# Top-k attention and a SwiGLU FFN in one kernel: units by query tile, FFN blocks of 256 tokens across batches, V stationary, mask and SwiGLU products on GpSimd, tanh for sigmoid

## The chip, the core and the metric

The kernel runs on one NeuronCore of a Trainium2 chip. Its engines are TensorE (PE, with its weight loads listed as PEld), VectorE (DVE), ScalarE (ACT), GpSimd (POOL) and SyncE (SP), which here only issues DMAs. The metric is the device time of one execution in microseconds (us). Before the change it is 2606.95 us, the median of 3 runs (2606.77 to 2609.73).

## What is computed

Everything is float32. Attention over 8 batches, 8 heads, 576 tokens and 64 dimensions per head keeps the 32 largest scores of each row; its output, with the heads side by side, is a matrix x of 4608 tokens by 512, which goes through a SwiGLU block with 1536 hidden columns. The three FFN weights arrive as float64.

```python
scores = scale * np.matmul(q, k.transpose(0, 1, 3, 2))          # scale = 1/8
kth = np.partition(scores, -32, axis=-1)[..., -32:-31]
scores = np.where(scores >= kth, scores, -1e9)
attn = np.exp(scores - np.max(scores, axis=-1, keepdims=True))
attn = attn / (np.sum(attn, axis=-1, keepdims=True) + 1e-09)
x = np.matmul(attn, v).transpose(0, 2, 1, 3).reshape(4608, 512)
g = x @ w_gate
out = (g * (1.0 / (1.0 + np.exp(-g))) * (x @ w_val)) @ w_out
```

## The kernel before

**Units.** Attention goes by unit. A unit is one batch, one pair of heads and one tile of queries: four tiles of 128 queries (two heads, so 256 rows of 576 scores), and a last one of 64 queries, in which both heads share one tile of 128 rows. I call the first kind a full unit and the last kind a half unit. There are 160 units, 128 full and 32 half. The order is batch, pair of heads, tile of queries: a pair's five units follow each other (L188).

**One unit.** `scores` (L195) multiplies Q by K for the 512 main keys and the last 64 of each head, and ACT copies the scores from PSUM (L211). `select` (L214) finds the 32nd largest of each row with four MAX8 (L227) and three MATCH_REPLACE8 (L237) on DVE; POOL makes -scale*max (L229), ACT the exponential of every score (L231), and DVE zeroes what lies below the threshold (L240, one scalar_tensor_tensor per head: compare, then multiply). `turn` (L250) transposes the result on PE (L260, L266) and ACT copies it out (L261, L267). `values` (L275) multiplies it with V: the transposed weights of 128 queries are the stationary operand and 65 columns of V (64 and a column of ones, which gives the row's sum) are streamed past it (L287). DVE adds epsilon to the sum and inverts it (L295, L296), ACT scales (L299), PE transposes once more (L303) and ACT copies into xT (L306).

**FFN.** `feed` (L316) is a generator for one batch in three blocks of 192 tokens (BLK). Each of the 12 slabs of hidden columns is one piece: four products with w_gate into PSUM and a copy by ACT (L336); after all 12 the sigmoid on ACT over 2304 columns (L338) and one product of that size on POOL (L339); then 12 pieces with w_val, multiplied on DVE straight from PSUM (L341). Last come the output products (L348), with 512 streamed columns each. A block of 192 tokens is cut at the 128-token tiles, so every block has one output tile of 128 tokens and one of 64.

**Order of the work.** The main loop (L368) emits for each unit n: scores of n+1, selection of n, transposes of n-1, four pieces of `feeds` (L381), and the values of n-2. A batch's FFN enters `feeds` when its last unit is done, so it runs beside the units of the next batch. At the start `feeds` holds `weights` (L127): 72 pieces which each load 128 by 256 float64 numbers by a DMA from POOL's queue (L91) and round them on POOL, ACT and DVE (L97 to L122), also four per unit. `load` (L145) issues 12 DMAs for a pair from SP's queue; `prep` (L158) transposes K and Q, and POOL copies V beside its ones (L184, L185).

The program order sets priorities and not the order on an engine: the tile framework lays the order of each engine out ahead of time by priority and expected readiness, and the order then stays fixed. In the trace PE runs two gate or value products between the transposes of L260 and L266, which the program has later.

```python
sc = work.tile([P, 2, S], ...)      # 2 buffers; PSUM: ps_s 2 x 2 banks, ps_t 2, ps_f 2
per_unit = 4                        # pieces of FFN, or of weights, behind each unit
```

Of the kernel before, what the change touches and what calls it, by code (L numbers as in the profile page):

```python
# [9 lines left out]
ALU = mybir.AluOpType  # L10
# [6 lines left out]
LOWEST = -3.4028234663852886e38  # L17
EPS = 1.0e-9
BLK = 192
WP = 256  # L20
HUGE = 122880.0  # 1151 << 20 as a float32's bits
LEAST = 3.4332275390625e-05  # 897 << 20 as a float32's bits
# [3 lines left out]
def kernel(  # L26
# [10 lines left out]
    """Top-k attention, then SwiGLU, in float32 throughout.  # L37

    Attention goes by unit (batch, pair of heads, tile of queries): the scores
    of both heads, the 32nd largest of each row by four rounds of max and three  # L40
    of match_replace, exp(s - max) zeroed below it, and the product with the
    values, whose last column of ones gives the sum of the row. A pair of heads
    is one 128-row slab of x transposed, which is what the first products of
    the FFN want. The FFN of a batch runs between the units of the next one.

    The tokens of a head are laid out as 4 tiles of the tokens 4 p + j, j < 4,
    and a last one of 64, so that each partition reads 1 KiB in one piece.

    The weights come in float64 and are rounded to float32 here, on their bits,
    while the first batch's attention runs.  # L50
    """
# [9 lines left out]
    DE = D + 1  # L61
    scale = 1.0 / float(D) ** 0.5
    assert D == 64 and R == 64 and H * D == DM and DM == 512 and S % BLK == 0

    consts = ctx.enter_context(tc.tile_pool(name="consts", bufs=1))
    ld = ctx.enter_context(tc.tile_pool(name="ld", bufs=2))
    work = ctx.enter_context(tc.tile_pool(name="work", bufs=2))
    small = ctx.enter_context(tc.tile_pool(name="small", bufs=4))
    conv = ctx.enter_context(tc.tile_pool(name="conv", bufs=2))
    ffn = ctx.enter_context(tc.tile_pool(name="ffn", bufs=2))  # L70
    ps_s = ctx.enter_context(tc.tile_pool(name="ps_s", bufs=2, space=PSUM))
    ps_t = ctx.enter_context(tc.tile_pool(name="ps_t", bufs=2, space=PSUM))
    ps_f = ctx.enter_context(tc.tile_pool(name="ps_f", bufs=2, space=PSUM))
# [3 lines left out]
    NV = 3  # L77
    vbufs = []
    for i in range(NV):
        vt = consts.tile([P, 2, J + 1, DE], FP32, name=f"v{i}")  # L80
        nc.gpsimd.memset(vt[:], 1.0)
        vbufs.append(vt)
# [4 lines left out]
    def rounded(src, dst):  # L87
        """Float64 bits, [low, high] word by word, to the nearest float32."""
        n = dst.shape[1]
        w = conv.tile([P, n, 2], I32, tag="w", name="w")  # L90
        nc.gpsimd.dma_start(w[:], src.bitcast(I32).rearrange("p (f t) -> p f t", t=2))  # L91
        yield
        low, high = w[:, :, 0], w[:, :, 1]
        # As float32 numbers the high words have the order of the float64 ones.
        # Held to float64 exponents up to 1151, float32's infinity.
# [4 lines left out]
        size = conv.tile([P, n], FP32, tag="size", name="size")  # L100
        nc.scalar.activation(size[:], hi[:], AF.Abs)
        # From 896 to 1151 the exponents' top bit and low seven are float32's exponent.
# [13 lines left out]
        half = conv.tile([P, n], I32, tag="half", name="half")  # L116
# [4 lines left out]
        # Zero below the exponent 897, that of float32's least normal number.  # L121
# [5 lines left out]
    def weights():  # L127
        pieces = []
        for src, dst in ((w_gate, wg), (w_val, wv), (w_out, wo)):
            for c in range(dst.shape[1]):  # L130
                for f in range(0, dst.shape[2], WP):
                    pieces.append(
                        rounded(src[c * P : (c + 1) * P, f : f + WP], dst[:, c, f : f + WP])
                    )
        for n in range(len(pieces) + 1):
            if n < len(pieces):
                next(pieces[n])
            if n > 0:
                next(pieces[n - 1], None)
                yield  # L140
# [4 lines left out]
    def load(i):  # L145
        b, hp = pairs[i]
        raw[i] = {}
        for name, src in (("k", k), ("q", q), ("v", v)):
            t = ld.tile([P, J + 1, 2, D], FP32, tag=name, name=f"{name}_in")
            for hh in range(2):  # L150
                head = src[b, 2 * hp + hh]
                nc.sync.dma_start(
                    t[:, 0:J, hh, :], head[0:JP].rearrange("(p j) d -> p j d", j=J)
                )
                nc.sync.dma_start(t[0:R, J, hh, :], head[JP:S])
            raw[i][name] = t

    def prep(i):  # L158
        """K and Q transposed, both heads in one slab; V beside its ones."""
        got = raw.pop(i)  # L160
        slabs = []
        for name in ("k", "q"):
            slab = work.tile([P, S], FP32, tag=name + "T", name=name + "T")
            main = ps_t.tile([P, 512], FP32, tag="t", name="main")
            for c in range(J):
                nc.tensor.transpose(
                    main[:, c * P : (c + 1) * P],
                    got[name][:, c].rearrange("p h d -> p (h d)"),
                    ident[:],
                )  # L170
            nc.scalar.copy(slab[:, 0:JP], main[:])
            slabs.append(slab)
        last = ps_t.tile([P, 512], FP32, tag="t", name="last")
        for n, name in enumerate(("k", "q")):
            nc.tensor.transpose(
                last[:, n * R : (n + 1) * R],
                got[name][0:R, J].rearrange("p h d -> p (h d)"),
                ident[0:R, 0:R],
            )
        for n, slab in enumerate(slabs):  # L180
            nc.scalar.copy(slab[:, JP:S], last[:, n * R : (n + 1) * R])
        vb = vbufs[i % NV]
        to = vb[:, :, :, 0:D].rearrange("p h j d -> p j h d")
        nc.gpsimd.tensor_copy(to[:, 0:J], got["v"][:, 0:J])  # L184
        nc.gpsimd.tensor_copy(to[0:R, J], got["v"][0:R, J])  # L185
        preps[i] = (*slabs, vb)

    units = [(i, qt) for i in range(len(pairs)) for qt in range(J + 1)]  # L188
    state = {}

    def n_tiles(qt):
        """The last 64 queries of both heads share one tile."""
        return 1 if qt == J else 2

    def scores(n):  # L195
        i, qt = units[n]
        kT, qT, _ = preps[i]
        sc = work.tile([P, 2, S], FP32, tag="sc", name="sc")
        ql = R if qt == J else P
        tiles = [(0, 1)] if qt == J else [(0,), (1,)]  # L200
        for t, heads in enumerate(tiles):
            ps = ps_s.tile([P, 1024], FP32, tag="s", name="s")
            for x, hh in enumerate(heads):
                d = slice(hh * D, (hh + 1) * D)
                for k0, k1 in ((0, 512), (512, S)):
                    nc.tensor.matmul(  # L206
                        ps[x * R : x * R + ql, k0:k1],
                        qT[d, qt * P : qt * P + ql],
                        kT[d, k0:k1],
                    )  # L210
            nc.scalar.copy(sc[:, t, :], ps[:, 0:S])  # L211
        state[n] = dict(sc=sc)
# [209 lines left out]
```

## Time and profile before

| | |
|---|---|
| time, median of 3 runs | 2606.95 us |
| span of the profiled execution, first to last instruction | 2599.7 us |
| median run less that span | 7.2 us |
| busy share of PE, DVE, ACT, POOL | 89%, 74%, 37%, 12% |
| mean granted clock of TensorE | 0.976 |
| first unit's first MAX8 | at 15.8 us |
| first MAX8 of each batch | 15.8, 365, 637, 927, 1217, 1508, 1798, 2088 us |
| last rounded weight written | at 356 us |
| HBM traffic over the span | 47.19 MB read, 9.44 MB written |

Of the profiled execution only the span is known; its own time from launch to end is not listed, so the 7.2 us between the span and the median run stand for what lies around it. In the profile a busy share counts the time in which an engine has an instruction in flight. Matmuls overlap in their pipeline, so the mean duration of one (349 ns at 192 columns) is not what one costs in a row of them; for that the start-to-start times are used. A float32 product shows as two MATMUL records. Batches 2 to 6 follow each other every 290.0 us.

### The profile page before, as it was taken

The page shows a single profiled execution, that of the slowest core. Times are in us where ns is not written, and L with a number is a line of the kernel's source. Part 1 is how long each engine was busy: PE and PEld are TensorE (multiplying, and loading weights), DVE is VectorE, ACT ScalarE, POOL GpSimd, SP SyncE. Part 2 cuts the span into 40 slices and gives each one's busy share as a digit, 9 for nine tenths or more (in the row PEclk, how much of TensorE's full clock was granted, in tenths as well). Part 3 has the DMA queues.
Part 4 walks back from the last instruction along what each step waited for, and adds up shares of the span by engine and source line. Part 5 has one row for each costly group of instructions (what it writes and reads, how often), then busy time and mean ns, then how long its engine had stood idle before and what let it go on. Part 6 is the DMA issues. An engine that isn't in the chain of part 4 may idle for free. (4 is left out here: it accounts for less than half of the span.)

```text
span 2599.7 us, 33003 instructions
## 1 busy us (share of the span) xinstructions
PE 2325.9 (89%) x12160; PEld 1733.6 (67%) x12160; DVE 1911.0 (74%) x4136; ACT 971.4 (37%) x2108; POOL 314.3 (12%) x473
## 2 busy tenths in 40 slices
PE   5656579999999999999999999999999999999898
PEld 3444456667767668668667668668668667677666
DVE  7889898778787788769777788769768788765000
ACT  3333234335334335334434434434425434423111
POOL 3434321011011011011001001001101101000000
PEclk9999998999999999999999999999999999999999
DMA  3222110000000000000000000000000000000000
GB/s 100 61 67 71 62 34 14 21 17 19 21 19 17 20 7 19 16 21 15 21 20 15 21 16 19 7 20 15 21 20 15 21 16 1 7 7 5 7 5 11
DMA packets 128032, 58.75 MB, mean 23 GB/s; under 512 B 118656, under 2 KB 118656, under 8 KB 127872
## 3 DMA queue, kind: packets, MB, share of 16 engines
q1 hardware_dynamic: 122112, 37.78, 6.0%
q0 software_dynamic: 5760, 18.88, 2.4%
q8 instruction: 96, 1.57, 0.3%
q14 instruction: 64, 0.52, 0.1%
HBM read 47.19 MB, written 9.44 MB: 22 GB/s over the span
## 5 line engine op out<-in xcount | busy, mean ns | idle before, releaser
L227 DVE MAX8 m<-rest 128x8 f32<-128x576 f32 x864 | 619.8, 748 | 1.7
L326 PE MATMUL f<-xT,wv 128*128 128x192 f32 x2304 | 459.3, 349 | 76.1 <-DVE h L341 75.9
L348 PE MATMUL f<-wo,h 128*128 128x512 f32 (+1 forms) x1152 | 506.6, 595 | 0.0
L326 PEld LDWEIGHTS f<-xT,wv 128*128 128x128 f32 x2304 | 400.0, 203 | 99.0 <-DVE h L341 85.0
L287 PE MATMUL av<-v,et 128*128 128x65 f32 (+3 forms) x3200 | 455.4, 287 | 3.2 <-ACT et L261 3.0
L287 PEld LDWEIGHTS av<-v,et 128*128 128x128 f32 (+3 forms) x3200 | 417.4, 195 | 58.1 <-issue 14.1
L326 PE MATMUL f<-xT,wg 128*128 128x192 f32 x2304 | 419.6, 331 | 6.5 <-ACT g L336 6.5
L237 DVE MATCH_REPLACE8 rest<-m,rest 128x576 f32<-128x576 f32 x576 | 424.5, 742 | 0.0
L326 PEld LDWEIGHTS f<-xT,wg 128*128 128x128 f32 x2304 | 370.8, 191 | 22.1 <-ACT g L336 10.7
L348 PEld LDWEIGHTS f<-wo,h 128*128 128x128 f32 (+1 forms) x1152 | 183.0, 163 | 291.2 <-issue 288.1
L206 PE MATMUL s<-kT,qT 64*128 64x64 f32 (+3 forms) x1280 | 297.9, 483 | 84.3 <-ACT sc L211 84.1
L211 ACT COPY sc<-s 128x576 f32<-128x576 f32 x288 | 182.1, 642 | 438.1 <-PE s L206 323.4
L295 DVE TENSOR_SCALAR rinv<-av 128x2 f32<-128x2 f32 (+1 forms) x160 | 25.0, 156 | 358.2 <-PE av L287 351.2
L206 PEld LDWEIGHTS s<-kT,qT 64*128 64x128 f32 (+1 forms) x1280 | 154.2, 193 | 184.3 <-ACT sc L211 88.8
L231 ACT ACTIVATE e<-sc,bias 128x576 f32<-128x576 f32 x288 | 213.3, 771 | 166.8 <-POOL bias L229 166.3
L240 DVE SCALAR_TENSOR_TENSOR e<-sc,m,e 128x576 f32<-128x576 f32 x288 | 273.2, 981 | 2.0
L341 DVE TENSOR_TENSOR h<-h,f 128x192 f32<-128x192 f32 x288 | 96.9, 348 | 227.3 <-POOL h L339 134.6
L227 DVE MAX8 m<-sc 128x8 f32<-128x576 f32 x288 | 212.4, 749 | 35.3 <-ACT sc L211 33.9
L229 POOL TENSOR_SCALAR bias<-m 128x2 f32<-128x2 f32 (+1 forms) x160 | 34.8, 217 | 1480.2 <-DVE m L227 1344.1
L237 DVE MATCH_REPLACE8 rest<-m,sc 128x576 f32<-128x576 f32 x288 | 212.8, 742 | 0.0
L260 PE MATMUL main<-ident,e 128*128 128x128 f32 x1152 | 186.2, 302 | 14.5 <-DVE e L240 12.2
L356 ACT COPY o<-f 128x512 f32<-128x512 f32 (+1 forms) x48 | 28.0, 583 | 439.7 <-PE f L348 439.7
(52 smaller groups left out, 1565.9 us busy)
## 6 DMA issues: line engine op xcount, KB each, us to landing
k_in<-in_k_dram SPq DMA_DIRECT2D x64, 128.0 KB, 2.6
q_in<-in_q_dram SPq DMA_DIRECT2D x64, 128.0 KB, 2.6
v_in<-in_v_dram SPq DMA_DIRECT2D x64, 128.0 KB, 2.6
w<-in_moe_w_gate_dram POOLq DMA_DIRECT2D x24, 256.0 KB, 3.0
w<-in_moe_w_val_dram POOLq DMA_DIRECT2D x24, 256.0 KB, 3.0
w<-in_moe_w_out_dram POOLq DMA_DIRECT2D x24, 256.0 KB, 3.1
out_dram<-o SPq DMA_DIRECT2D x24, 256.0 KB, 2.2
out_dram<-o SPq DMA_DIRECT2D x24, 128.0 KB, 2.3
```

The lines of the kernel that those rows point to most:

```text
L206: nc.tensor.matmul(ps[x * R : x * R + ql, k0:k1], qT[d, qt * P : qt * P + ql], kT[d, k0:k1],)
L211: nc.scalar.copy(sc[:, t, :], ps[:, 0:S])
L227: nc.vector.max(m8[t], cur[t])
L229: nc.gpsimd.tensor_scalar_mul(bias[:, 0:nt], m[:, 0:nt, 0], -scale)
L231: nc.scalar.activation(e[:, t, :], sc[:, t, :], AF.Exp, bias=bias[:, t : t + 1], scale=scale)
L237: nc.vector.match_replace(rest[:], m8[t], cur[t], LOWEST)
L240: nc.vector.scalar_tensor_tensor(out=e[:, t, :], in0=sc[:, t, :], scalar=m[:, t, TOP_K - 1 : TOP_K], in1=e[:, t, :], op0=ALU.is_ge, op1=AL ...
L260: nc.tensor.transpose(main[:, cs], e[:, t, cs], ident[:])
L287: nc.tensor.matmul(av[0:ql, hh, :], et[0:kl, t, c, q0 : q0 + ql], vb[0:kl, hh, c, :], start=(c == 0), stop=(c == J),)
L326: nc.tensor.matmul(ps[:], w[:, c, m * P : (m + 1) * P], x[:, c, c0 : c0 + BLK], start=(c == 0), stop=(c == KC - 1),)
L341: nc.vector.tensor_mul(h[:, m, :], h[:, m, :], product(wv, m)[:])
L348: nc.tensor.matmul(ps[0:n, :], h[:, m, s0 - c0 : s0 - c0 + n], wo[:, m, :], start=(m == 0), stop=(m == MC - 1),)
```

## The change

- Units run by batch, query tile, pair of heads: the four pairs of a tile follow each other, and `prep` of all four pairs falls in a batch's first four units.
- The FFN takes blocks of 256 tokens, numbered over the whole 4608 tokens (18 blocks), and a block may start as soon as its tokens are done for all four pairs (`done`). It is emitted in 18 pieces: six pairs of slabs with gate and value pieces (16 MATMUL records of 256 columns each), and two output tiles of 128 tokens in three pieces each (8 records of 512 columns). A running credit of 2.3 pieces per full unit and 1.15 per half unit, held to 3.0, paces it. By the loop's count 304 of the 324 pieces are emitted within it and 20 after it.
- Weight pieces: eight per unit, loaded from SP's queue, in another order.
- `scores`: PSUM in one buffer of three banks; the last 64 keys of both heads sit in a block-diagonal tile (`klast`), so a full unit has one product of 128 keys for them.
- `select`: after all rounds POOL makes -scale*max, then a penalty of -3e38 where the score is below the threshold (one tensor_scalar per head, is_lt and mult), and adds the scores; ACT takes the exponential and the row's sum with it; DVE adds epsilon and inverts; ACT scales e. The scalar_tensor_tensor on DVE is gone.
- `values`: V is stationary (64 columns), the transposed weights are streamed (128 columns), and the result lands as x transposed: the extra transpose and the scaling behind it are gone. `values` runs one unit behind instead of two.
- SwiGLU: ACT takes tanh(g/2), g/2, 1 + tanh and a copy of the value product; two products on POOL per pair of slabs. Nothing of it is left on DVE.
- A pair's load has 14 DMAs instead of 12.

```diff
-BLK = 192
+BLK = 256
...
-    ps_s = ctx.enter_context(tc.tile_pool(name="ps_s", bufs=2, space=PSUM))
+    ps_s = ctx.enter_context(tc.tile_pool(name="ps_s", bufs=1, space=PSUM))
...
-    ps_f = ctx.enter_context(tc.tile_pool(name="ps_f", bufs=2, space=PSUM))
+    ps_f = ctx.enter_context(tc.tile_pool(name="ps_f", bufs=3, space=PSUM))
...
-        nc.gpsimd.dma_start(w[:], src.bitcast(I32).rearrange("p (f t) -> p f t", t=2))
+        nc.sync.dma_start(w[:], src.bitcast(I32).rearrange("p (f t) -> p f t", t=2))
...
-    units = [(i, qt) for i in range(len(pairs)) for qt in range(J + 1)]
+    units = [(b, qt, hp) for b in range(B) for qt in range(J + 1) for hp in range(NHP)]
...
+            for hh, d in enumerate(halves):
+                nc.tensor.matmul(ps[:, 1024 * hh : 1024 * hh + JP], slab[d, qs], slab[d, 0:JP])
+            nc.tensor.matmul(ps[:, JP : JP + P], slab[:, qs], kl[:])
+            nc.scalar.copy(sc[:, 0 : JP + P], ps[:, 0 : JP + P])
+            nc.scalar.copy(sc[:, JP + P : 2 * S], ps[:, 1024:1536])
...
+        bias = small.tile([P, 2], FP32, tag="bias", name="bias")
+        nc.gpsimd.tensor_scalar_mul(bias[:, 0:nh], m[:, 0:nh, 0], -scale)
+        for t, hs in enumerate(heads):
+            nc.gpsimd.tensor_scalar(
+                e[:, hs], sc[:, hs], m[:, t, TOP_K - 1 : TOP_K], FAR, ALU.is_lt, ALU.mult
             )
+        every = slice(0, nh * S)
+        nc.gpsimd.tensor_tensor(e[:, every], e[:, every], sc[:, every], ALU.add)
+        tot = small.tile([P, 2], FP32, tag="tot", name="tot")
+        for t, hs in enumerate(heads):
+            nc.scalar.activation(
+                e[:, hs], e[:, hs], AF.Exp, bias=bias[:, t : t + 1], scale=scale,
+                accum_out=tot[:, t : t + 1],
+            )
+        nc.vector.tensor_scalar_add(tot[:, 0:nh], tot[:, 0:nh], EPS)
+        nc.vector.reciprocal(tot[:, 0:nh], tot[:, 0:nh])
+        for t, hs in enumerate(heads):
+            nc.scalar.mul(e[:, hs], e[:, hs], tot[:, t : t + 1])
...
+        if not last:
+            nc.tensor.matmul(av[:], vl[:], et[:, J, :], start=True, stop=False)
+        for c in range(J + 1 if last else J):
+            kl = R if c == J else P
+            for hh in range(2):
...
                 nc.tensor.matmul(
+                    av[hh * R : (hh + 1) * R, 0:ql],
+                    vt[0:kl, c, hh, :],
+                    moving,
...
+        for s in range(MS):
+            h = ffn.tile([P, 2, BLK], FP32, tag="h", name="h", bufs=MS + 1)
+            half = ffn.tile([P, 2, BLK], FP32, tag="gv", name="half_g", bufs=3)
+            ps = product(wg, s)
+            nc.scalar.activation(h[:], ps[:], AF.Tanh, scale=0.5)
+            nc.scalar.mul(half[:], ps[:], 0.5)
+            nc.scalar.add(h[:], h[:], 1.0)
+            nc.gpsimd.tensor_mul(h[:], h[:], half[:])
+            yield
+            val = ffn.tile([P, 2, BLK], FP32, tag="gv", name="val", bufs=3)
+            nc.scalar.copy(val[:], product(wv, s)[:])
+            nc.gpsimd.tensor_mul(h[:], h[:], val[:])
+            hs.append(h)
+            yield
...
+    for n in range(NU + 1):
+        if n + 1 < NU:
+            b, qt, hp = units[n + 1]
+            i = b * NHP + hp
+            if qt == 0:
+                if i + 1 < len(pairs) and hp < NHP - 1:
+                    load(i + 1) if i + 1 not in raw else None
+                if i not in preps:
+                    prep(i)
+            if qt == J and i + NHP < len(pairs) and hp < 2:
+                load(b * NHP + NHP + hp)
+            scores(n + 1)
+        if n < NU:
+            select(n)
+            credit += 1.15 if units[n][1] == J else 2.3
+        if n >= 1:
+            turn(n - 1)
+        for half in range(2):
+            if half and n >= 1:
+                values(n - 1)
+            for _ in range(4):
+                next(weight, None)
+            while credit >= (1 - half) * 1.15 + 1 and piece():
+                credit -= 1
+        credit = min(credit, 3.0)
+    while piece():
+        pass
```

## The prediction

> **What bounds the kernel now.** I read the page's busy shares and its 40 slices first.
>
> ```profile
> PE 2325.9 (89%) x12160; PEld 1733.6 (67%) x12160; DVE 1911.0 (74%) x4136; ACT 971.4 (37%) x2108; POOL 314.3 (12%) x473
> ...
> PE   5656579999999999999999999999999999999898
> ...
> DVE  7889898778787788769777788769768788765000
> ```
>
> From slice 6 on PE is full, to the end; before that DVE leads, while the weights are rounded and no FFN exists yet. The table of stretches puts numbers to three stages.
>
> ```profile
> 130.00:300.00 170.00, 104.31 (x369) 75.78 (x368) 149.88 (x377) 54.61 (x128) 66.95 (x121) 1.00 0.23 67
> ...
> 900.00:1500.00 600.00, 567.68 (x3158) 428.33 (x3154) 470.58 (x976) 250.81 (x538) 51.72 (x65) 0.98 0.08 18
> ...
> 2420.00:2600.00 180.00, 158.16 (x684) 117.47 (x682) 12.46 (x36) 21.36 (x42) 15.10 (x3) 0.94 0.02 7
> ```
>
> The columns after the length are busy us of PE, PEld, DVE, ACT and POOL. Start: DVE 88%. Middle: PE 95%, DVE 78%. Tail: PE alone, on the last batch's FFN. So the middle and the tail cost what PE's instructions cost, and the groups by line, shapes apart, say which.
>
> ```profile
> L326 PE MATMUL f<-xT,wv 128*128 128x192 f32 x2304 | 459.3, 349 | 76.1 <-DVE h L341 75.9
> L287 PE MATMUL av<-v,et 128*128 128x65 f32 x2048 | 302.0, 294 | 3.2 <-ACT et L261 3.0
> L240 DVE SCALAR_TENSOR_TENSOR e<-sc,m,e 128x576 f32<-128x576 f32 x288 | 273.2, 981 | 2.0
> L348 PE MATMUL f<-wo,h 128*128 128x512 f32 x576 | 255.9, 595 | 0.0
> L348 PE MATMUL f<-wo,h 128*64 128x512 f32 x576 | 252.3, 594 | 0.0
> L339 POOL TENSOR_TENSOR h<-h,g 128x2304 f32<-128x2304 f32 x24 | 122.8, 5117 | 293.3 <-ACT h L338 183.5 <-issue 55.4 <-PE f L326 54.4
> L97 POOL TENSOR_SCALAR hi<-w 128x256 f32<-128x256 f32 x72 | 30.9, 430 | 74.2 <-DMA w<-in_moe_w_out_dram 24.0 <-DMA w<-in_moe_w_gate_dram 22.0 <-DMA w<-in_moe_w_val_dram 21.5
> ```
>
> Half of L348's time goes to 64-token tiles at the full price (594 against 595 ns). From starts of consecutive records I take PE's spacings: 163 ns at 192 streamed columns, 429 at 512, 109 for a 128-column transpose, 112 for 65 columns behind 128-column weights, 60 behind 64-column ones. So a column costs 0.84 ns, but a record no less than its weight load.
>
> **A check of these spacings on the kernel before**, per batch: FFN 3 x (192 x 0.163 + 48 x 0.429) = 155.7 us; a full unit 1.25 (scores, eight records) + 10 x 0.109 + 2.7 (20 value records with their switches) + 0.17 (L303) = 5.2, a half unit 3.7, a prep 1.1: 16 x 5.2 + 4 x 3.7 + 4 x 1.1 = 102. Sum 258. The trace's batches follow every 290.0 us, which is 1.124 times that; the clock (0.976), exposed weight loads and the waits make the rest. The waits, longest first, show the third of it that has names:
>
> ```profile
> DVE rinv L295 <- PE av L287: 351.2, 124, 22.3
> ...
> DVE h L341 <- POOL h L339: 134.6, 10, 43.9
> ...
> PE s L206 <- ACT sc L211: 84.1, 22, 7.5
> PE f L326 <- DVE h L341: 75.9, 24, 6.7
> ...
> PE xps L303 <- ACT x L299: 61.7, 61, 2.7
> ```
>
> DVE waits for PE, not the other way round, except around L341. The timeline shows that exception:
>
> ```profile
> 1298.92 5.63 DVE L240 SCALAR_TENSOR_TENSOR e<-sc,m,e 128x576 f32<-128x576 f32 x1
> ...
> 1298.63 5.30 POOL L339 TENSOR_TENSOR h<-h,g 128x2304 f32<-128x2304 f32 x1 [8.47 <-ACT h L338]
> ...
> 1306.18 5.49 PE L326 MATMUL f<-xT,wv 128*128 128x192 f32 x16 [3.96 <-DVE h L341]
> ```
>
> An instruction of 0.8 us took 5.63 because POOL's product ran; PE stood 3.96 us in the end. Beside the same L339, MAX8 kept 746 ns and MATCH_REPLACE8 737.
>
> **PE after, per batch.** FFN: 2.25 blocks x (192 x 0.215 + 48 x 0.429) = 2.25 x 61.9 = 139.2 us, 16.5 less, nearly all from output tiles that are now full. Full unit: scores 1.25 again (four 512-column records still run two by two on the array's halves, then two of 128 columns instead of four of 64); nine transposes, 0.98; values 18 records. For these the trace has no row: V's two heads use the same rows and different columns. Upper end: one after the other at 128 columns, 18 x 0.109 = 2.05 with a switch. Lower end: by the half unit's score records (64 rows by 64 columns, the other half 13 ns later) pairs run together: 2 x 0.109 + 8 x 0.109 + switches = 1.25. I take 1.25, since in every row where the records of a product use disjoint parts of the array they overlap, and keep 2.05. Full unit 3.48, half unit 1.13 + 0.55 + 0.9 = 2.58, prep 1.0. Sum: 139.2 + 16 x 3.48 + 4 x 2.58 + 4 = 209.2, or 223.6 with V unpaired (half unit +0.4). At 1.124: 235 and 251 us per batch instead of 290.
>
> The array's part of this can be weighed against a rule. L287's records take about 205 ns instead of 112 where 128-row and 64-row weights alternate, four times in a unit before. The Trainium skill, TensorEngine Tiling (Array Packing), Key Properties, says that a change of tiling mode drains TensorE, and that different tiles run in parallel. By the first half V stationary pays two drains per unit, by the second the pairs overlap; the sum by the page is the lower end above.
>
> **The others after, per batch.** DVE: a full unit has eight MAX8 at 0.667 and six MATCH_REPLACE8 at 0.727 with their value loads, 9.7, and the two small operations 0.15: 9.85. Half 5.0. Batch 178. L240 (0.73 back to back, more beside POOL) and L341 (0.26) are gone. ACT, whole run: score copies 160, exponentials 203, the new scaling at the exponential's price 198, et 193, x 45, prep 45, weights 27, SwiGLU 18 x (24 x 0.545 + 2 x 0.58) = 257: 1128, or 141 per batch, from 971. The 43 table loads of 1.28 us go if tanh and Exp share a table; if not, 216 switches cost ACT 277 us, still under PE. POOL: the two-input row gives 2.2 ns per element, so the sum over 1152 costs 2.66 and a SwiGLU product 1.3; the penalty is a tensor_scalar, 0.70 by L97 (215 ns for two columns, 430 for 256), 1.28 if it ran at the two-input rate, which is its upper end. Full unit 0.22 + 1.40 + 2.66 = 4.28, half 2.35; with 18 x 12 x 1.3 and the weights (85) about 990 us, or 124 per batch. All three stay under 235, so PE covers them.
>
> New waits: inverting the sums on DVE waits for POOL's 4.3 us and ACT's 1.4; behind it stand the next unit's MAX8, for which PE waits a unit later. The cover is DVE's slack, (235 - 178)/18 = 3.2 us per full unit, plus the fixed order placing next MAX8 ahead of it, as it places other work between today. The exponential likewise holds ACT's queue; three PSUM buffers of the FFN give PE 10 us. One buffer for scores costs nothing while its copies are done a unit earlier. `prep` moved to just before its scores hides behind the running unit's 9.85.
>
> That lock has a rule too: SBUF, State Buffer, section SBUF: two separate sides, in the Trainium skill says that GpSimd and a DVE operation with two SBUF inputs or in a two-port mode exclude each other for a whole instruction. By it the small addition on the sums, now read from SBUF, would wait for POOL: half the time, about 1.1 us, 90 us of DVE's slack in all, so the sum by it is the same.
>
> **Start.** FFN can begin after eight units instead of 20. Nine units carry all 72 weight pieces: 9.85 + 8 x 1.47 (their DVE rows) = 21.6 us of DVE, at the 93% that the same arithmetic gives for today's 18.5 us per unit, 23.4; x 9 + 16 = 227. On SP the weights' issues (0.60 each) now stand behind 28 loads, so the first piece comes at about 21 us instead of 6, when DVE has its first unit; a unit's 8 + 14 issues take 14 us. I take 235. PE has done 35 of its 1674 us by then.
>
> **Sum.** 235 + (8 x 209.2 - 35) x 1.124 = 235 + 1842; units that get no FFN piece run at DVE's pace, by the emission count 15 us; the last unit's chain (POOL, ACT, PE) and the last copy and store 12. Span 2104, with 7 around it **2111 us**. Unpaired V adds 8 x 14.4 x 1.124 = 129. The factor may lie between 1.07 (half of today's waits gone) and 1.20 (POOL's and ACT's fixed places fit worse): -89 and +125. Range 2020 to 2330.
>
> **Rivals.** (1) *DVE waits in program order.* The sum's inversion stands before the next MAX8 on DVE: 9.85 + 4.28 + 1.40 + 0.3 for the handovers = 15.8 us per full unit, 8.35 per half: 119 x 15.8 + 32 x 8.35 + start 264 + tail 84 + 7 = 2502. For: DVE already waits 351 us at L295. Against: it waits for a late PE there, and the orders do interleave. (2) *The same chain with the penalty at the two-input price*: +1.16 per full unit, 2502 + 167 = 2669, **slower** than before. It decides from 16.5 us per full unit. A penalty of over 6 us each would do the same through POOL's sum; no row suggests it. (3) *The waits around L341 and L303 were most of the overhead*: factor 1.0 to 1.06, 1910 to 2010. (4) *Tanh brings table loads*, so the change doesn't do what it says: 1.28 us per switch in the path of half the gate products, some 100 us, 2210; inside the range.
>
> **Chances.** Forecast with its ends and rival 4: 0.80. Below 2020: 0.05. Rival 1 from 2330 up: 0.09. Slower: 0.05. The rest within 0.2%, about what a measurement of this kernel can tell from no change: 0.01. Faster 0.94.
>
> **What would show it.** Batches 235 us apart; L348's group at 864 records; V's records in pairs a few ns apart (or 109 ns: +129); PE over 90% busy from about 235 us on, with DVE near 75%. Wrong if DVE's waits for ACT at the new inversion exceed 3 us per unit, if PE stands at PSUM waiting for ACT, or if the penalty costs over 1.3 us.

## The result and the profile after

The changed kernel takes 2757.53 us (median of 4 runs, 2757.09 to 2759.35) against 2608.34 (2606.77 to 2611.61) for the kernel before: 1.058 times as long, 95% interval 1.0554 to 1.0601. The forecast was 2111 us, so 646 us have to be explained. The profiled execution took 2757.09 us with a span of 2755.3 and a mean granted clock of 0.857, where the kernel before had 0.976.

The page after, shares of the span, then slices:

```profile
PE 2094.8 (76%) x9888; PEld 1398.0 (51%) x9888; DVE 1603.6 (58%) x3560; ACT 1134.3 (41%) x2493; POOL 1417.5 (51%) x984
...
PE   4256668777878788878877777787888778877789
...
DVE  6888865664556555655555554565545555556540
```

No engine is full. PE has 9888 records for 12160 and is busy 231 us less, but its slices show sevens and eights where the kernel before had nines. DVE, at sevens before, shows fives. ACT's total is within 1% of the forecast (1134 for 1128); POOL's is not (1417 for about 990). The stretch in the middle, with the columns as before (length; busy us of PE, PEld, DVE, ACT, POOL; granted clock):

```profile
900.00:1500.00 600.00, 474.14 (x2292) 318.30 (x2292) 332.23 (x729) 254.92 (x562) 305.56 (x191) 0.87 0.07 16
```

PE has fallen from 568 to 474 of 600 us, DVE from 471 to 332, and the clock from 0.98 to 0.87. So everybody waits. The waits say for whom (total us, times, longest):

```profile
ACT e L257 <- POOL e L254: 689.9, 156, 10.4
DVE tot L261 <- ACT e L257: 649.8, 138, 11.2
...
DVE m L240 <- ACT sc L224: 290.8, 87, 15.4
PE etps L277 <- ACT et L278: 273.0, 73, 9.7
```

ACT's exponential waits for POOL's sum, DVE's inversion for ACT's exponential, PE for ACT's copies. The wait on DVE is 649.8 us over 160 units, some 4 us each; the prediction had named 3 as the point from which it would be wrong. The groups give POOL's prices:

```profile
L250 POOL TENSOR_SCALAR e<-sc,m 128x576 f32<-128x576 f32 x288 | 638.9, 2227 | 609.0 <-DVE m L240 464.7
...
L254 POOL TENSOR_TENSOR e<-e,sc 128x1152 f32<-128x1152 f32 x128 | 335.0, 2617 | 9.1
```

The sum is as priced (2.62 us, 2.66 taken), and so is the SwiGLU product (1.27 in its groups L365 and L369, 1.3 taken). The penalty is 2.23 us, where 0.70 was taken and 1.28 was the upper end. One unit in the timeline (start, us, engine, instruction, in brackets the idle time before it and its releaser):

```profile
1299.23 4.41 POOL L250 TENSOR_SCALAR e<-sc,m 128x576 f32<-128x576 f32 x2
...
1303.73 2.61 POOL L254 TENSOR_TENSOR e<-e,sc 128x1152 f32<-128x1152 f32 x1
...
1306.37 0.77 ACT L257 ACTIVATE e<-e,bias 128x576 f32<-128x576 f32 x1 [7.49 <-POOL e L254]
...
1308.03 0.17 DVE L261 TENSOR_SCALAR tot<-tot 128x2 f32<-128x2 f32 x1 [9.21 <-ACT e L257]
...
1311.32 0.69 ACT L224 COPY sc<-s 128x640 f32<-128x640 f32 x1
...
1312.11 1.42 DVE L240 MAX8 m<-sc 128x8 f32<-128x576 f32 x2 [3.70 <-ACT sc L224]
1312.37 0.78 ACT L278 COPY et<-etps 128x512 f32<-128x512 f32 x2
...
1313.03 0.69 PE L277 MATMUL etps<-ident,e 128*128 128x128 f32 x2 [8.05 <-ACT et L278]
```

In this unit the time goes as follows. ACT stands 7.49 us at the head of its queue for POOL. Behind that exponential stand the copies of the next unit's scores (L224) and of transposes that PE had finished at 1303.7 (L278). DVE stands 9.21 us at the inversion, then 3.70 more for the score copy, and PE 8.05 us for the other copy. It is one of the worse units: all eight of the next unit's MAX8 come after its inversion. That is so in 26 of the 128 full units, which hold 240 us of the wait there; in the other 102 two to four of the eight come first, and the wait is shorter. Batches follow each other every 322.8 us (290.0 before, 235 forecast).

### The profile page after: what moved, and what is told of

Its sections match the earlier page's. It is cut to its first block, busy times and chain, and to the rows that moved or that the text cites. A ratio compares the mean times of both kernels' runs of the same rounds, so it can differ in the third digit from the quotient of the medians.

```text
span 2755.3 us, 28809 instructions
## 1 busy us (share of the span) xinstructions
PE 2094.8 (76%) x9888; PEld 1398.0 (51%) x9888; DVE 1603.6 (58%) x3560; ACT 1134.3 (41%) x2493; POOL 1417.5 (51%) x984
## 3 DMA queue, kind: packets, MB, share of 16 engines
q8 instruction: 78, 1.28, 0.2%
## 4 chain that ended last, share of the span: by engine, by line
POOL 34%; DVE 26%; PE 15%; ACT 14%; issue 8%; DMA 2%; SPq 0%; POOLq 0%; DVEq 0%; ACTq 0%
POOL e L250 17%; POOL e L254 13%; DVE m L240 11%; DVE rest L243 11%; ACT e L257 7%; PE f L348 7%; PE o_ps L375 3%; PE av L304 2%; ACT e L264 2%; PE etps L277 1%; POOL h L365 1%; DMA w<-in_moe_w_val_dram 1%; POOL bits L130 1%; POOL h L369 1%; PE s L222 1%
## 5 line engine op out<-in xcount | busy, mean ns | idle before, releaser
L250 POOL TENSOR_SCALAR e<-sc,m 128x576 f32<-128x576 f32 x288 | 638.9, 2227 | 609.0 <-DVE m L240 464.7
L240 DVE MAX8 m<-rest 128x8 f32<-128x576 f32 x864 | 619.8, 749 | 2.1
L257 ACT ACTIVATE e<-e,bias 128x576 f32<-128x576 f32 x288 | 221.3, 769 | 689.9 <-POOL e L254 689.9
L277 PE MATMUL etps<-ident,e 128*128 128x128 f32 (+1 forms) x1312 | 243.7, 319 | 318.7 <-ACT et L278 273.0
L375 PE MATMUL o_ps<-wo,h 128*128 128x512 f32 x864 | 451.0, 658 | 0.0
L348 PE MATMUL f<-xT,wg 128*128 128x256 f32 x1728 | 443.7, 405 | 9.3 <-ACT xT L319 9.3
L348 PE MATMUL f<-xT,wv 128*128 128x256 f32 x1728 | 442.0, 402 | 0.9 <-ACT half_g L363 0.9
L240 DVE MAX8 m<-sc 128x8 f32<-128x576 f32 x288 | 206.3, 751 | 367.4 <-ACT sc L224 290.8
L261 DVE TENSOR_SCALAR tot<-tot 128x2 f32<-128x2 f32 (+1 forms) x160 | 28.2, 176 | 649.8 <-ACT e L257 649.8
L254 POOL TENSOR_TENSOR e<-e,sc 128x1152 f32<-128x1152 f32 (+1 forms) x160 | 379.8, 2374 | 11.2
L277 PEld LDWEIGHTS etps<-ident,e 128*128 128x128 f32 (+1 forms) x1312 | 173.0, 161 | 407.4 <-ACT et L278 321.6
L304 PE MATMUL av<-et,v 128*64 128x128 f32 (+2 forms) x2688 | 253.7, 324 | 26.9 <-ACT et L278 26.6
L375 PEld LDWEIGHTS o_ps<-wo,h 128*128 128x128 f32 x864 | 168.0, 211 | 160.2 <-issue 157.9
L365 POOL TENSOR_TENSOR h<-h,half_g 128x512 f32<-128x512 f32 x108 | 137.6, 1274 | 215.6 <-ACT h L364 215.6
L369 POOL TENSOR_TENSOR h<-h,val 128x512 f32<-128x512 f32 x108 | 137.5, 1273 | 197.2 <-ACT val L368 190.2
L264 ACT ACTIVATE e<-e,tot 128x576 f32<-128x576 f32 x288 | 210.6, 771 | 57.1 <-DVE tot L262 56.3
L278 ACT COPY et<-etps 128x512 f32<-128x512 f32 (+1 forms) x448 | 196.1, 473 | 86.1 <-PE etps L277 85.5
```

What stands on the lines that cost most here:

```text
L240: nc.vector.max(m[:, t, 8 * r : 8 * r + 8], cur[:, hs])
L250: nc.gpsimd.tensor_scalar(e[:, hs], sc[:, hs], m[:, t, TOP_K - 1 : TOP_K], FAR, ALU.is_lt, ALU.mult)
L254: nc.gpsimd.tensor_tensor(e[:, every], e[:, every], sc[:, every], ALU.add)
L257: nc.scalar.activation(e[:, hs], e[:, hs], AF.Exp, bias=bias[:, t : t + 1], scale=scale, accum_out=tot[:, t : t + 1],)
L264: nc.scalar.mul(e[:, hs], e[:, hs], tot[:, t : t + 1])
L277: nc.tensor.transpose(ps[0:kl, c * P : (c + 1) * P], e[:, k0 : k0 + kl], ident[:])
```

## The experiments

Three theories stood. **A1**: the loss is DVE standing at the inversion. **A2**: the loss is ACT standing at the exponential with PE's and DVE's copies behind it. **B**: it is POOL's price, whoever waits. The measured times of all whole kernels, with the ratio to the kernel before, the mean granted clock, the us per batch (a fifth of the time from the third batch's first MAX8 to the eighth's) and the two waits in us:

| kernel | us | ratio, 95% interval | clock | batch | ACT exp. for POOL | DVE inversion for ACT |
|---|---|---|---|---|---|---|
| the change | 2757.53 | 1.0578, 1.0554 to 1.0601 | 0.857 | 322.8 | 690 | 650 |
| stt | 2099.86 | 0.8054, 0.8035 to 0.8074 | 0.951 | 237.4 | 10 (bias) | none |
| const | 2596.45 | 0.9965, 0.9945 to 0.9984 | 0.876 | 304.8 | 559 | none |
| late | 2543.87 | 0.9766, 0.9739 to 0.9792 | 0.890 | 295.3 | 525 | 448 |
| fastpen | 2341.05 | 0.8981, 0.8948 to 0.9015 | 0.923 | 266.2 | 406 | 350 |
| pen2 | 3304.04 | 1.2675, 1.2644 to 1.2706 | 0.802 | 391.7 | 1235 | 1163 |
| mask_alone | 2916.65 | 1.1193, 1.1166 to 1.1219 | 0.941 | 324.3 | 701 | none |
| pen_dve | 2299.02 | 0.8818, 0.8800 to 0.8837 | 0.925 | 263.2 | 384 | 275 |
| late2 | 2552.35 | 0.9789, 0.9768 to 0.9809 | 0.888 | 295.2 | 527 | 429 |
| fast_const | 2279.88 | 0.8731, 0.8698 to 0.8765 | 0.921 | 261.9 | 323 | none |
| stt2 | 2094.47 | 0.8033, 0.8017 to 0.8049 | 0.953 | 236.3 | 8 (bias) | none |
| free | 2217.23 | 0.8493, 0.8479 to 0.8508 | 0.927 | 246.2 | none | 28 |

### stt: the mask back on DVE, the rest of the change kept

```diff
+            if r == 0:
+                nc.gpsimd.tensor_scalar_mul(bias[:, 0:nh], m[:, 0:nh, 0], -scale)
+                for t, hs in enumerate(heads):
+                    nc.scalar.activation(
+                        e[:, hs], sc[:, hs], AF.Exp, bias=bias[:, t : t + 1], scale=scale
+                    )
...
-            nc.gpsimd.tensor_scalar(
-                e[:, hs], sc[:, hs], m[:, t, TOP_K - 1 : TOP_K], FAR, ALU.is_lt, ALU.mult
-            )
...
-        nc.gpsimd.tensor_tensor(e[:, every], e[:, every], sc[:, every], ALU.add)
...
+            nc.vector.scalar_tensor_tensor(
+                out=e[:, hs], in0=sc[:, hs], scalar=m[:, t, TOP_K - 1 : TOP_K],
+                in1=e[:, hs], op0=ALU.is_ge, op1=ALU.mult, accum_out=tot[:, t : t + 1],
```

> The changed kernel with the mask alone put back: exponential on ACT after the first MAX8, compare-and-multiply on DVE (which now also gives the row's sum), inversion and scaling as in the change. Theory A (the chain POOL penalty 2 x 2.2, POOL sum 2.6, ACT exponential 1.9 us stands in series with DVE's rounds): the series goes, DVE gets 2 x 0.73 us more per full unit (11.5), PE sets the pace again: 2100 to 2300 us, DVE's wait at the inversion under 100 us, PE clock back at 0.95 or more. Rival B (the rest of the change is slow by itself: one score buffer, ACT's SwiGLU work, V stationary): stays above 2500 us.

2099.86 us, 237.4 per batch. Its middle stretch:

```profile
900.00:1500.00 600.00, 572.16 (x3111) 393.50 (x3108) 550.76 (x1214) 337.85 (x668) 104.45 (x122) 0.99 0.08 18
```

PE is at 95% again and the clock at 0.99, with DVE at 92% although it has the mask back. So all 646 us, and 11 more, belong to the mask's new place and to the later exponential that comes with it. The other parts of the sum come out close here, though DVE does more than in the forecast and POOL less (2099.86 for 2111; 237.4 for 235 per batch; the tenth unit starts at 238.7 us for 235).

### const and late: DVE's wait taken away, or moved

In const the inversion is gone and the weights are scaled by a tile of ones. In late the exponential, the inversion and the scaling are emitted after the next unit's rounds, in front of the transposes.

```diff
-        nc.vector.tensor_scalar_add(tot[:, 0:nh], tot[:, 0:nh], EPS)
-        nc.vector.reciprocal(tot[:, 0:nh], tot[:, 0:nh])
...
-            nc.scalar.mul(e[:, hs], e[:, hs], tot[:, t : t + 1])
+            nc.scalar.mul(e[:, hs], e[:, hs], one[:, t : t + 1])
```

> The changed kernel without the addition of epsilon and the inversion; e is scaled by ones instead of by the inverted sum, so the output is not normalised. Only DVE's wait for ACT goes, POOL and ACT do the same work. Theory A1 (DVE's wait of 650 us for the exponential is what stretches the units): 2150 to 2400 us. Rival A2 (ACT's queue stands at the exponential, 690 us, and holds the copies that PE and the next unit's scores need; DVE's wait is a shadow of it): 2600 to 2760 us, with DVE now waiting for score copies instead.

```diff
+        state[n]["mask"] = (e, bias, heads, nh)
+
+    def finish(n):
+
+        e, bias, heads, nh = state[n].pop("mask")
...
         if n >= 1:
+            finish(n - 1)
             turn(n - 1)
```

> Same instructions as the change; exponential, inversion and scaling of a unit are emitted after the next unit's rounds, so that DVE's inversion and ACT's exponential stand one unit later in their queues. Theory A (places in the fixed queues, not POOL's sum of work, make the time; POOL has 10.2 us of work per full unit): 2200 to 2450 us, the waits ACT on POOL and DVE on ACT fall from 690 and 650 us below 200 each. Rival C (POOL's latency or its load itself bounds): above 2600 us.

const takes 161 us less than the change, late 214; neither landed where a theory had put it (const lies 4 us below A2's range). DVE's stand in const has moved to the score copies:

```profile
DVE m L242 <- ACT sc L226: 688.4, 89, 28.3
ACT e L259 <- POOL e L256: 558.6, 132, 8.6
```

Without an inversion DVE stands 688 us for the copies behind ACT's exponential. So the inversion, taken away alone, is worth a quarter of the loss (161 of 646), and the rest stays with ACT or POOL. In late all eight of the next unit's MAX8 come before the inversion in 98 of the 128 full units, and these wait 54 us there in all; 27 units still have none of them before it and wait 275 us. ACT still stands 525 us for POOL.

### micro: what POOL asks for each form

The forms, dearest first; the kernel runs them eight times in another order.

```python
ts(pen[:], sc[:], th, FAR, ALU.is_lt, ALU.mult)
ts(sub_min[:], sc[:], th, 0.0, ALU.subtract, ALU.min)
ts(cmp_imm[:], sc[:], 0.25, FAR, ALU.is_lt, ALU.mult)
ts(cmp_one[:], sc[:], th, None, ALU.is_lt)
ts(mul_one[:], sc[:], 0.5, None, ALU.mult)
nc.gpsimd.tensor_tensor(both[:], sc[:], x[:], ALU.add)
ts(mul_add[:], sc[:], th, 0.5, ALU.mult, ALU.add)
ts(clamp[:], sc[:], 0.25, -0.25, ALU.min, ALU.max)
nc.vector.tensor_scalar(pen_v[:], sc[:], th, FAR, ALU.is_lt, ALU.mult)
```

> Computes nothing of the reference: eight rounds of eight forms on POOL, 128 x 576 float32, and the penalty once per round on DVE. If the compare is what costs: every form with is_lt near 2.2 us, subtract-min, clamp and multiply-add near 0.7. If the per-partition scalar costs: is_lt with an immediate near 0.7, subtract-min and multiply-add with a pointer near 2.2. If two operations cost: the single ones are cheaper. The sum of two tiles 1.4 us; the penalty on DVE 0.35 to 0.7.

Most of the groups, in the same order (busy us, mean ns of one):

```profile
L69 POOL TENSOR_SCALAR pen<-sc,m 128x576 f32<-128x576 f32 x8 | 18.0, 2253 | 0.8
L75 POOL TENSOR_SCALAR sub_min<-sc,m 128x576 f32<-128x576 f32 x8 | 17.8, 2220 | 0.0
...
L73 POOL TENSOR_SCALAR cmp_one<-sc,m 128x576 f32<-128x576 f32 x8 | 14.0, 1747 | 0.6
L81 POOL TENSOR_SCALAR mul_one<-sc 128x576 f32<-128x576 f32 x8 | 13.3, 1667 | 0.0
...
L79 POOL TENSOR_SCALAR mul_add<-sc,m 128x576 f32<-128x576 f32 x8 | 6.0, 754 | 0.0
L77 POOL TENSOR_SCALAR clamp<-sc 128x576 f32<-128x576 f32 x8 | 5.4, 670 | 0.1
L85 DVE TENSOR_SCALAR pen_v<-sc,m 128x576 f32<-128x576 f32 x8 | 5.3, 731 | 0.0
```

One opcode with one shape costs 0.67 to 2.25 us on POOL. The pairs minimum-maximum and multiply-add are fast; a multiplication alone takes 1.67. Neither the compare nor the pointer operand makes the price by itself: subtract-and-minimum is as dear as the compare (2.22), a compare with a constant too (2.14), and multiply-add with a pointer is cheap. The sum of two tiles (1.40) lies between. L97, from which the 0.70 came, is a minimum-maximum pair. The Trainium skill, GPSIMD Engine Reference, section 4.1 (Engine selection), calls one-input work on this engine "roughly line-rate": true of the two fast pairs, which stand level with DVE's 0.73, and not of the others, at 2.3 to 3.1 times that. The measurement decides.

### fastpen, pen2 and pen_dve: the price alone

fastpen puts a multiply-add (which masks nothing) in the penalty's place. pen2 issues the penalty twice. pen_dve issues it on DVE and leaves the sum on POOL.

```diff
-                e[:, hs], sc[:, hs], m[:, t, TOP_K - 1 : TOP_K], FAR, ALU.is_lt, ALU.mult
+                e[:, hs], sc[:, hs], m[:, t, TOP_K - 1 : TOP_K], 0.5, ALU.mult, ALU.add
```

> The changed kernel with a multiply-and-add in the penalty's place (0.75 us on POOL in the forms' measurement instead of 2.25); it masks nothing, so the softmax runs over all keys. It gives the penalty the price that the prediction took, with everything else and every dependency of the change in place. Theory P (only the price was wrong; at 0.75 the chain fits into the covers that the prediction named): 2100 to 2250 us. Theory S (the series DVE, POOL, ACT costs its full length at any price): 2400 to 2550 us. In between, 2280 to 2380, if each us of POOL's chain costs a us per unit: 2757 less 128 x 3.0 and 32 x 1.5.

```diff
+            nc.gpsimd.tensor_scalar(
+                e[:, hs], sc[:, hs], m[:, t, TOP_K - 1 : TOP_K], FAR, ALU.is_lt, ALU.mult
+            )
```

> The changed kernel with the penalty done twice: 4.4 us more on POOL per full unit, 2.2 per half unit, the same values. If POOL's chain is on the path in every unit: 128 x 4.4 + 32 x 2.2 = 634 us more, 3390 us. If half of it is hidden: about 3070. If POOL's chain is hidden and DVE's or ACT's order makes the time: under 2850 us.

```diff
-            nc.gpsimd.tensor_scalar(
+            nc.vector.tensor_scalar(
```

> The changed kernel with the penalty on DVE (0.73 us each by the forms' measurement) and the sum left on POOL. The chain after the last round is 1.3 us of DVE, 2.6 of POOL, 1.9 of ACT instead of 4.4, 2.6 and 1.9. Theory P: PE's pace, 2100 to 2200 us. One us for one us: 2757 less 128 x 3.0 and 32 x 1.5, that is 2320 us. Theory S: above 2400 us.

The group in the penalty's place in fastpen:

```profile
L250 POOL TENSOR_SCALAR e<-sc,m 128x576 f32<-128x576 f32 x288 | 216.1, 759 | 642.8 <-DVE m L240 487.1 <-PE o_ps L375 42.6 <-PE etps L277 28.1
```

In the change's order, a microsecond on POOL costs almost a microsecond of the kernel. With the penalty at 0.76 us the time falls by 416 us, for 423 us less of POOL (288 x 1.47; POOL's total is then 989 us, the forecast's 990); doubled, it rises by 547 for 639 us more. Off POOL it falls by 459. POOL is no full engine in any of these (34 to 62% busy), so this is length on a path and not load. At the price that I had taken, the kernel still misses the forecast by 230 us: the mis-sized price is not the whole of it.

### mask_alone: the kernel before, with the change's mask only

```diff
-                nc.gpsimd.tensor_scalar_mul(bias[:, 0:nt], m[:, 0:nt, 0], -scale)
-                for t in range(nt):
-                    nc.scalar.activation(
-                        e[:, t, :], sc[:, t, :], AF.Exp, bias=bias[:, t : t + 1], scale=scale
-                    )
...
+            nc.gpsimd.tensor_scalar(
+                e[:, t, :], sc[:, t, :], m[:, t, TOP_K - 1 : TOP_K], FAR, ALU.is_lt, ALU.mult
+            )
+        nc.gpsimd.tensor_tensor(e[:, 0:nt, :], e[:, 0:nt, :], sc[:, 0:nt, :], ALU.add)
...
-            nc.vector.scalar_tensor_tensor(
...
+            nc.scalar.activation(
+                e[:, t, :], e[:, t, :], AF.Exp, bias=bias[:, t : t + 1], scale=scale
```

> The kernel before with the mask of the change alone: after all rounds POOL's penalty and sum, then the exponential on ACT; DVE's compare-and-multiply is gone; the row's sum still comes from the column of ones, so DVE waits for no exponential. Theory A1 (DVE's wait at the inversion stretches the units): PE still sets the pace, 2570 to 2640 us. Theory A2 (ACT's queue standing at the exponential is enough): 2680 to 2900 us.

2916.65 us, 17 above A2's range: 309 us lost in the old kernel too, though its inversion still reads PE's sum and not ACT's.

```profile
ACT e L241 <- POOL e L239: 700.6, 137, 15.1
DVE rinv L291 <- PE av L283: 620.7, 110, 22.3
```

ACT stands 701 us at the exponential, as in the change (690). This agrees with A2: the loss needs no wait of DVE for ACT's sum. It doesn't exclude a part of DVE, whose old wait for PE at the inversion has grown from 351 to 621 us. The clock there is 0.941.

### late2, fast_const and stt2: what is left

late2 goes further than late: transposes and values run two units behind the selection, with three buffers of the weights. fast_const joins fastpen and const. stt2 gives stt the two units' distance.

```diff
-        if n >= 1:
-            turn(n - 1)
+        if 1 <= n <= NU:
+            finish(n - 1)
+        if n >= 2:
+            turn(n - 2)
...
-            if half and n >= 1:
-                values(n - 1)
+            if half and n >= 2:
+                values(n - 2)
```

> The change's own instructions, with the exponential, the inversion and the scaling emitted one unit later than the penalty, and transposes and values two units behind the selection (three buffers of e, one of the rounds' scratch). The rounds of the next unit stand ahead of the inversion in program order, and PE asks for the scaled weights a whole unit later. If the loss is only in where the waiting instructions stand in the queues of DVE and ACT, POOL's 7.1 us per full unit with the products' 2.6 or so fits beside PE's 13: 2100 to 2300 us, DVE's wait at the inversion under 100 us. If the handover from POOL holds ACT's queue wherever it stands, since copies for PE are behind it: over 2450, near late's 2543.87.

> The cheap penalty (0.75 us, it masks nothing) and no inversion (the exponentials are scaled by ones): both remaining waits but ACT's at POOL are out. With the cheap penalty alone 2341.05. If what is left at that price is DVE standing at the inversion: 2110 to 2200, at the forecast. If ACT's queue standing at the exponential is enough for it: 2270 to 2341. At the dear price leaving out the inversion gave 161 us of 646, a quarter; a quarter of the 230 left here would be 2283.

> The version with the mask back on DVE and an early exponential (2099.86 us), with transposes and values two units behind. If waits around the inversion and the scaling still cost there: 2040 to 2085. If PE is simply full (89% in the profile, 237 us per batch): 2090 to 2110.

late2 (2552.35) gains nothing over late (2543.87): more distance between the selection and PE's work doesn't help while the exponential still waits for POOL at the head of ACT's queue (527 us). fast_const shows that at the cheap price DVE's inversion is worth 61 us (2341.05 to 2279.88) of the 230, again about a quarter; 169 remain, with ACT standing 323 us for POOL. stt2 (2094.47) cannot be told from stt (2099.86), as the intervals of their ratios overlap: PE is busy 89% of the span in both.

### free: the dear penalty kept on POOL, but behind the exponential and the inversion

If ACT's and DVE's queues are the loss, it must go when POOL keeps its work and only the order of the operations changes: exponential first, then inversion and scaling, and POOL's mask last, as a product. As the row's sum is then taken before the mask, free is an experiment and no replacement.

```diff
+            if r == 0:
...
+                nc.vector.tensor_scalar_mul(bias[:, 0:nh], m[:, 0:nh, 0], -scale)
+                for t, hs in enumerate(heads):
+                    nc.scalar.activation(
+                        e[:, hs], sc[:, hs], AF.Exp, bias=bias[:, t : t + 1], scale=scale,
+                        accum_out=tot[:, t : t + 1],
+                    )
...
             nc.scalar.mul(e[:, hs], e[:, hs], tot[:, t : t + 1])
+        pen = work.tile([P, 2 * S], FP32, tag="pen", name="pen", bufs=1)
+        for t, hs in enumerate(heads):
+            nc.gpsimd.tensor_scalar(
+                pen[:, hs], sc[:, hs], m[:, t, TOP_K - 1 : TOP_K], 1.0, ALU.is_ge, ALU.mult
+            )
+        every = slice(0, nh * S)
+        nc.gpsimd.tensor_tensor(e[:, every], e[:, every], pen[:, every], ALU.mult)
```

> POOL keeps the change's work: the compare at its price (2.2 us a head) and a product over all 1152 columns in the place of the sum (some 2.6 us), 7.1 us per full unit; ACT keeps the exponential with its row sum, DVE the inversion, ACT the scaling. Only the order differs: the exponential reads the scores right after the first round (its bias is made on DVE), the inversion and the scaling follow, and POOL masks the scaled weights last. So neither ACT nor DVE stands for POOL; only PE's transposes do. The sums are taken over all keys before the mask, so the weights are not normalised over the 32 kept ones. If the loss is instructions of ACT and DVE standing for POOL with others' work queued behind them: 2100 to 2250 us, with ACT at the exponential waiting less than 60 us in all. If it is POOL's load as such (7.1 us more per unit before PE can go on, its lock on DVE, its products late): over 2450.

2217.23 us. The compare costs what it did (2223 ns for 2227), and the waits have other names:

```profile
ACT e L259 <- DVE tot L257: 257.0, 125, 6.3
DVE m L240 <- ACT sc L224: 240.8, 84, 15.5
...
PE etps L279 <- POOL e L266: 88.5, 24, 10.9
```

POOL does 638 us of compares as in the change (it is 62% busy), and 540 of the 646 us are gone. ACT's 690 us at the exponential are gone; it waits 37 us for POOL at the score copies, and for DVE 257 us at the scaling and 86 at the exponential, more than the 60 that I had expected there. DVE waits 28 us at the inversion, where it had waited 650. PE waits 89 us for POOL. So the loss was neither POOL's load nor the dear price as such, but that ACT and DVE stood for POOL at the head of their queues. The 106 us that remain above the forecast have more than one candidate. PE's wait is one. Another is the bias, which free makes on DVE:

```profile
L244 DVE TENSOR_SCALAR bias<-m 128x2 f32<-128x2 f32 x128 | 116.8, 913 | 0.0
```

The 22 of all 160 that run beside no POOL instruction take 156 ns each, the 58 beside POOL's product 1.41 us on average. No run takes these parts of the 106 us apart.

## Why the prediction was wrong

**The step that failed** is the paragraph on new waits: "The cover is DVE's slack, (235 - 178)/18 = 3.2 us per full unit, plus the fixed order placing next MAX8 ahead of it", and for ACT "three PSUM buffers of the FFN give PE 10 us". The chain itself was seen, with the right engines; its cover was argued from other work that is interleaved in the kernel before. The runs show what happened in its place: part of the next MAX8 do come before the inversion (two to four of eight in 102 of the 128 full units), but the copies that PE and DVE need stand behind the exponential. ACT stood 690 us there for POOL, and DVE 650 at the inversion. PSUM buffers for the FFN didn't help, since PE stood at the transposes (L277, 273 us), which need ACT's copies too. ACT was priced by its load alone, 1128 us under PE's, and an engine that is 41% busy cost the most.

**The second step that failed** is the price "0.70 by L97", with "1.28 if it ran at the two-input rate, which is its upper end". It measured 2.23. The row had the right opcode and the right engine but another pair of operations, and the dearer price lay above the end that I had called its upper one. Rival 2 had the series and the sign ("**slower** than before"), with a chance of 0.05 for slower, and its 2669 us lie within 4% of the result. That is in part luck: it took 1.28 for the penalty, and it put the stand at DVE's inversion alone, which const shows to be worth 161 of the 646 us. (Its sum adds the dearer price to 128 full units where rival 1 counts 119; that is 10 us.) With the inversion gone DVE stands for the copies behind the exponential instead, so that the series stays. Its threshold was 16.5 us per full unit; the trace has 322.8 / 18.1 = 17.8 (a half unit counted as 0.53). Fully in series with the measured prices it would be 9.85 + 0.22 + 2 x 2.21 + 2.61 + 1.4 + 0.3 = 18.8, so by this estimate only about 1 us per unit of the chain was covered.

**How the two steps share the 646 us** depends on the order in which they are mended. Price first: 416 by the price, 230 left. Stands first: 540 by the order at the full price, 106 left. The two shares overlap, since a long operation costs what it lasts only where somebody stands for it.

**What held**, by stt, in which only the mask is undone: 235 us per batch (237.4 measured), the start (238.7 us for 235), the factor 1.124 (237.4 / 209.2 = 1.135). V's heads run in pairs: in the changed kernel's timeline the two records of a pair start some 7 ns apart, and the 16 records of a unit's V take 1.10 us (from 1317.87 to 1318.97 us). L375 has 864 records. The 7 us around the span are 1.8 (2757.09 less 2755.3). tanh and Exp brought no further table loads (one of 1.28 us in the whole run), which settles rival 4. ACT's load was right to 1%. The small addition on the sums, for which a wait of about 1.1 us was weighed, took 176 ns on average, but only 10 of the 160 fell beside a POOL instruction at all; four of these took 0.56 to 0.72 us, and in free the small operations of DVE beside POOL's product are slowed more.

**The clock** was in the sum only through the factor 1.124, taken over from the kernel before with its 0.976. Around the unit shown, the stretches of 4 us (columns as before, the clock behind POOL) read:

```profile
1304.00:1308.00 4.00, 0.98 (x5) 0.53 (x3) 0.00 (x0) 1.62 (x4) 3.56 (x2) 1.00 0.00 0
1308.00:1312.00 4.00, 0.00 (x0) 0.00 (x0) 0.34 (x2) 3.50 (x7) 0.50 (x1) 0.76 0.00 0
1312.00:1316.00 4.00, 2.97 (x9) 2.58 (x10) 3.89 (x8) 1.74 (x5) 1.00 (x2) 0.50 0.00 0
1316.00:1320.00 4.00, 4.00 (x29) 3.29 (x28) 4.00 (x11) 0.85 (x2) 1.27 (x1) 0.89 0.04 10
```

PE stops at 1305, the granted clock is 0.76 and then 0.50 when PE starts again, and full speed is back some 4 us later. This agrees with the Trainium skill, TensorE: Matmul & The Clock Gate, section "What's actually happening", which has the clock halved after an idle window of about 3.4 us and restored after one that is busy. It is why the same 9888 records are 2095 us busy in the change and 1870 in stt: in both, consecutive records of the gate and value products start 216 ns apart at the full clock and 427 ns at half of it (medians), and PE is busy at the half clock for 553 us in the change and 114 in stt. By half of these times, 277 and 57 us, the clock accounts for 220 of the 225 us. Over the runs of the table that keep the change's order of units, the clock mostly falls as the time grows, from 0.953 at 2094 us to 0.802 at 3304. The mean alone doesn't set a time: the runs of the kernel before lie within 0.6% of each other, with means from 0.919 to 0.976. Since the gaps come with the stands, I take the clock for an amplifier of them, and how much of the 646 us it adds is argued and not shown: no run has the gaps without the clock, or the clock without the gaps.

## What to carry to other kernels

Before an operation goes to a slow engine, ask which instruction on another engine will stand for its result, and what is queued behind that instruction; an engine that is 41% busy can cost the most in this way. Put the slow operation where only its last consumer waits for it: free keeps POOL's dear penalty and its pass over all columns, and is 540 us faster than the change. It doesn't compute the same, though; the version here that does, and is faster still, leaves the mask on DVE (stt). And a price is taken from a row with the same operations, not only the same opcode; without one, the range needs the dearest row of that engine at several times its rate, or a small measurement first.

## What was not expected of the hardware

- On POOL, a tensor_scalar over 128 x 576 float32 takes 0.67 us (minimum, maximum), 0.75 (multiply, add), 1.67 (multiply alone), 1.75 (compare alone), 2.22 (subtract, minimum) or 2.25 (compare, multiply); a sum of two tiles takes 1.40, less than a multiplication by a constant.
- An exponential with a row sum on ACT brings an ACTIVATION_READ_ACCUMULATOR of 187 ns behind it, 288 of them in the change.
- stt's compare-and-multiply on DVE takes 0.74 us from start to start at the median, and 1.74 at the 90th percentile (it lasts 0.81 us beside no POOL instruction, 1.26 on average beside a SwiGLU product): the wait for POOL's products that the kernel before showed around L240 is still there, and stt is the fastest version all the same, with stt2.
